# A gated mix of attention and GEGLU: the gate and up products each get a row tile of their own

## The chip, the cores and the metric

The kernel runs on one core of one Trainium2 chip. The metric is the device time of one execution in microseconds (us). Before the change three runs took 1230.1, 1230.26 and 1230.33 us, so the median is 1230.26 us. The core has a matrix engine (TensorE, PE in the profile, with its weight loads shown as PEld), a vector engine (VectorE, DVE), an activation engine (ScalarE, ACT), a general engine (GpSimd, POOL), a queue engine that issues most transfers (SyncE, SP), and two memories on the chip: SBUF, which every engine reads, and PSUM, eight banks into which PE accumulates.

## The reference

x has 2048 rows of 512 numbers. Everything is float32.

```python
g = sigmoid((x * gate_w).sum(-1, keepdims=True))
# attention: 32 query heads of 16, one key and one value head for all of them
q = heads(x @ wq);  k = x @ wk;  v = x @ wv
p = softmax(einsum("bhqd,bkd->bhqk", q, k) * 16 ** -0.5)
a = merge(einsum("bhqk,bkd->bhqd", p, v)) @ wo
# feed-forward, hidden width 1376
b = (gelu(x @ w_gate) * (x @ w_up)) @ w_down
out = g * a + (1 - g) * b
```

The softmax needs 2048 x 2048 exponentials for each of the 32 heads, and all of them go through ACT.

## The kernel before

**Tiles.** The 2048 rows are four groups of 512 (`tg`). The hidden width of the feed-forward is cut into 11 chunks of 128 (`NF`), so there are 44 chunks `n = 11 * tg + r`. Products in which accuracy matters are made from two float32r halves of each operand, high and low: one product is three matmuls, high by high, high by low and low by high. A split is a copy to float32r on DVE (line 186) and a subtraction on POOL (line 187).

**Prologue** (the first 79.5 us). The loads, the splits of x, and for every row group the query, key and value projections and chunk 0 of the feed-forward. The groups run in the order 1, 2, 3, 0. In the last of them (lines 434 to 467) PE makes four query blocks `pq`; for each, `post_q` takes a row maximum (line 272) and the low half (line 281) on DVE. The maxima meet in `pairmax` (lines 470 to 477), whose transposes `pm` stand in PE's queue, and its result `sh` is what the matmul `pb` (line 481) needs. Both are in PE's order ahead of everything that follows.

**Main part.** A step of attention is a score (two 51-row matmuls into one of three two-bank buffers, line 745), an exponential over 128 x 1024 on ACT (line 748) into one of 12 buffers `p`, and, for two scores together, the product with v (line 816, four column tiles of 32, here called a V). There are 1024 scores and 512 V. Between them PE works through jobs of the feed-forward: 39 gate jobs (gate and up of one chunk), 16 down jobs and 6 jobs of the output projection (`wo`). A job fills two PSUM banks: `z`, which is the third score buffer, and `y`.

**Two row tiles.** A job's matmuls contract 128 rows as two halves of 64 rows, one in the lower and one in the upper half of the array, and the two run side by side. `pair_mm` (lines 509 to 531) gives `z` to the lower tile and `y` to the upper tile in the first half of the job, and swaps them in the second. Between the halves stands a relay: a GpSimd nop (line 523) that waits for the last matmuls of the first half, and for which the first matmuls of the second half wait.

**The order of work** is a list written out by hand, `PLAN`, one line per job. H opens the job, F is one pair of its matmuls (Fk is k of them), S is a score into one of two buffers, Z a score into the third buffer (the one that `z` uses between H and R), V is one product with v, R reads the job's banks out, T queues the tanh of a gate job on ACT. The steps go out in this order, and each engine works its own queue in that order.

**Side work** sits in slots: after every third F, `slot` issues one waiting item on DVE and POOL, from `todo` (splits of weights and of x) or, when that is empty or in some slots of a first half, from `bg` (pieces of the softmax's division, `norm`). A gate job of 24 F has seven slots. Items issued in a job's slots stand in DVE's queue ahead of the job's own read-out, which is issued at R: lines 615 and 617 for a down job, line 541 and the GELU chain (lines 544 to 557) for a gate job.

**Batches.** A down job multiplies all chunks collected so far by `w_down`: after chunk 5 and after chunk 10 of each row group, two down jobs each (two blocks of 128 rows in a job), with 18 and 15 terms, so 36 and 30 F. The next row group's x is loaded in four pieces of 128 x 512 and split in the slots of the down jobs after chunk 10. Loads go from SP through a ring of four staging buffers (`st`).

## Time and profile before

| | |
|---|---|
| median of three runs | 1230.26 us |
| the profiled execution | 1230.25 us |
| its span in the trace | 1228.5 us |
| PE busy | 1222.3 us, 9742 matmuls |
| ACT busy | 1025.5 us |
| DVE busy | 545.6 us |
| POOL busy | 216.1 us |
| first score | 79.5 us after the span's start |

The profile shows one execution. The busy time of PE counts modelled ends of pipelined matmuls, so it is the distance between starts that tells what a step costs. A line of the timeline gives start, length, engine, line of the kernel, operation, output and inputs, and a count when equal neighbours are merged; in brackets stands the idle time of the engine before it, and what ended it. A line of a group ends in busy time, mean length of one in ns, and idle time before.

### The profile page before, as it was taken

The numbers are of one execution on the slowest core, as the hardware profiler recorded it, in microseconds if no ns is written. First come the engines' busy times: TensorE is split into PE (matmuls) and PEld (weight loads), VectorE is DVE, ScalarE is ACT, GpSimd is POOL, SyncE is SP. The second block draws the span as 40 slices with busy tenths as digits, with TensorE's granted clock in tenths as the row PEclk, the third lists the DMA queues.
The fourth block names the chain that finished last, engine by engine and source line by source line (L and its number), as shares of the span: only waits on it lengthen the run. The fifth ranks groups of instructions, "written<-read, shape, count | busy, mean of one in ns | idle before, by whom it ended". The sixth has DMA issues, their size and how long they took to land.

```text
span 1228.5 us, 23738 instructions
## 1 busy us (share of the span) xinstructions
PE 1222.3 (99%) x9742; PEld 670.2 (55%) x9742; DVE 545.6 (44%) x812; ACT 1025.5 (83%) x1127; POOL 216.1 (18%) x188
## 2 busy tenths in 40 slices
PE   9999999999999999999999999999999999999998
PEld 7865455555654555455555554654554555545545
DVE  7774423656245051545437152263626244144624
ACT  5459988988898888988888888889888898889883
POOL 5423101222121010212112020121311011012100
PEclk9999999999999999999999999999999999999999
DMA  8642201222121110112112120111211211002000
GB/s 333 215 132 57 67 7 51 66 61 71 33 66 48 44 32 23 52 54 77 56 35 58 48 67 15 47 43 51 83 41 49 74 49 32 23 27 66 15 1 35
DMA packets 39839, 73.91 MB, mean 60 GB/s; under 512 B 5488, under 2 KB 5744, under 8 KB 39728
## 3 DMA queue, kind: packets, MB, share of 16 engines
q1 hardware_dynamic: 39184, 71.32, 18.4%
q8 instruction: 77, 1.26, 0.4%
q0 software_dynamic: 256, 0.79, 0.2%
q10 hardware_dynamic: 288, 0.26, 0.1%
q14 instruction: 34, 0.28, 0.1%
HBM read 57.41 MB, written 14.94 MB: 59 GB/s over the span
## 4 chain that ended last, share of the span: by engine, by line
PE 93%; DVE 0%; ACT 0%; issue 0%
PE acc L816 38%; PE s L745 23%; PE z L515 20%; PE y L515 11%; PE wos L501 1%; PE u L501 0%; DVE acc L627 0%; ACT p L748 0%; PE wof L501 0%; DVE sq L545 0%; DVE sq L544 0%; DVE gs L541 0%; ACT sq L548 0%
## 5 line engine op out<-in xcount | busy, mean ns | idle before, releaser
L748 ACT ACTIVATE p<-s 128x1024 f32<-128x1024 f32 x1024 | 972.3, 1027 | 143.0 <-PE s L745 137.6
L816 PE MATMUL acc<-p,v 128*32 128x512 f32 x4096 | 485.0, 597 | 0.0
L745 PE MATMUL s<-Q,kp 51*128 51x512 f32 x2048 | 384.6, 415 | 0.1
L745 PEld LDWEIGHTS s<-Q,kp 51*128 51x128 f32 x2048 | 183.7, 184 | 215.7 <-ACT p L748 124.3
L816 PEld LDWEIGHTS acc<-p,v 128*32 128x32 f32 x4096 | 114.0, 109 | 250.6 <-issue 242.3
L187 POOL TENSOR_TENSOR gl<-st,gh 128x512 fp32r<-128x512 f32 x80 | 114.0, 1444 | 755.1 <-PE s L745 375.7
L515 PE MATMUL y<-xh,gh 64*128 64x512 f32 x312 | 125.7, 403 | 0.0
L515 PE MATMUL z<-xh,gh 64*128 64x512 f32 x312 | 125.7, 403 | 0.0
L515 PE MATMUL y<-xl,gh 64*128 64x512 f32 x312 | 122.4, 392 | 0.0
L515 PE MATMUL z<-xl,gh 64*128 64x512 f32 x312 | 122.2, 392 | 0.0
L515 PE MATMUL z<-xh,gl 64*128 64x512 f32 x312 | 121.8, 390 | 0.0
L515 PE MATMUL y<-xh,gl 64*128 64x512 f32 x312 | 121.7, 390 | 0.0
L541 DVE COPY gs<-z 128x512 f32<-128x512 f32 x39 | 27.0, 692 | 194.9 <-PE y L515 112.0
L187 POOL TENSOR_TENSOR dl<-st,dh 128x512 fp32r<-128x512 f32 x44 | 57.3, 1304 | 127.1 <-PE s L745 90.0
L515 PE MATMUL z<-dh,hh 64*128 64x512 f32 x176 | 69.5, 395 | 0.0
L515 PE MATMUL y<-dh,hh 64*128 64x512 f32 x176 | 69.5, 395 | 0.0
L515 PE MATMUL y<-dl,hh 64*128 64x512 f32 x176 | 69.0, 392 | 0.0
L515 PE MATMUL z<-dl,hh 64*128 64x512 f32 x176 | 68.8, 391 | 0.0
L515 PE MATMUL z<-dh,hl 64*128 64x512 f32 x176 | 68.7, 391 | 0.0
L515 PE MATMUL y<-dh,hl 64*128 64x512 f32 x176 | 68.7, 390 | 0.0
L515 PEld LDWEIGHTS z<-xh,gh 64*128 64x128 f32 x312 | 58.0, 186 | 15.0 <-POOLq L523 6.8
L515 PEld LDWEIGHTS z<-xl,gh 64*128 64x128 f32 x312 | 58.3, 187 | 8.1
(173 smaller groups left out, 1456.8 us busy)
## 6 DMA issues: line engine op xcount, KB each, us to landing
st<-wf SPq DMA_DIRECT2D x125, 256.0 KB
scr<-q SPq DMA_DIRECT2D x16, 512.0 KB
Q<-scr SPq DMA_DIRECT2D x64, 128.0 KB
Q<-scr SPq DMA_DIRECT2D x64, 64.0 KB
out<-acc SPq DMA_DIRECT2D x16, 256.0 KB
xr<-xT SPq DMA_DIRECT2D x6, 512.0 KB
st<-xT SPq DMA_DIRECT2D x12, 256.0 KB
xr<-xT SPq DMA_DIRECT2D x4, 256.0 KB
```

Of the source, the lines that this page charges most:

```text
L187: eng_l.tensor_sub(lo, src, hi)
L501: nc.tensor.matmul(ps, a, b, start=(first and q == 0), stop=(last and q == len(terms) - 1), skip_group_check=True)
L515: mm = nc.tensor.matmul(ps, a[rs], b[rs], start=(half == 0 and q == 0), stop=(half == 1 and q == len(X) - 1), skip_group_check=True)
L541: nc.vector.tensor_copy(gs, g)
L745: nc.tensor.matmul(ps[:, j * TG : (j + 1) * TG], kp[rs, kc * P : (kc + 1) * P], Q[u][rs, pr], start=True, stop=True)
L748: nc.scalar.activation(p, ps, AF.Exp, bias=0.0, scale=SCALE)
L816: nc.tensor.matmul(accp[u][32 * j : 32 * j + 32], vt[:, kc], pb[s, j // 2][:, (j % 2) * TG : (j % 2 + 1) * TG], start=(kc == 0), stop=(kc ...
```

## The change

- x lies in SBUF twice: for each row group four tiles `xd` hold the same 64 rows of x in partitions 0 to 63 and again in 64 to 127. The gate weights of a chunk lie in the lower 64 partitions, the up weights in the upper. A gate job then has 24 pairs in which the lower tile always makes gate (`z`) and the upper always makes up (`y`): `own_mm`, without the swap and without the relay. Down and wo jobs keep `pair_mm`.
- For row group 0 the doubled x is made in the prologue by 16 copies of 64 x 1024 between partitions, four behind each query block of the last group: one on ACT, one on DVE, two on POOL. For the other groups x is loaded doubled from a new input `xD`, in eight pieces instead of four, and split two pieces to a slot item: the first piece's low half on POOL, the second's on DVE.
- Down jobs come after chunks 3, 7 and 10, so six of them per row group with 24, 24, 24, 24, 18 and 18 F: 24 in all in place of 16.
- Fewer buffers for hidden tiles (`hh`, `hl`: 2 + 2 in place of 3 + 3) and for `w_down` (4 in place of 6). The 12 `p` buffers become 6 pairs. Pools of the prologue are closed in a new order.
- A new list, of 69 jobs. Those around the loads of the next x are shown.

```diff
 PLAN = [
     "t: S2",
...
+    "f: H F3 S F3 S F3 S F3 S F3 S F3 S F3 S F3 R S V S Z T S V6 S",
+    "f: H F3 S F3 S F3 S F3 S F3 S F3 S F4 S F2 R S V3 T S Z S V2 S",
+    "f: H F3 S F6 S2 F6 S F3 R S V Z S2 V3 S",
+    "f: H F3 S F6 S2 F6 S F3 R S V S Z S V3 S2 Z V3 S",
...
+    "f: H F3 S F3 S F3 S F3 S F3 S F3 S F3 S F3 R S V3 T Z S2 V2 S",
+    "f: H F3 S F6 S2 F6 S F3 R S V3 S",
+    "f: H F2 S F4 S F3 S F2 S F4 S F3 R S V Z S2 V3 S2 Z V3 S Z S V2 S",
...
+    "f: H F3 S F3 S F3 S F3 S F3 S F3 S F3 S F3 R S V S Z T S V4 S2 Z V3 S",
+    "f: H F S F8 S2 F7 S F2 R S V2 S Z S V2 S",
+    "f: H F3 S F6 S2 F9 R S2 V2 Z S2 V3 S",
...
+    def big(name):
+        return cp.tile([P, NC, TG], F32R, tag="xr", name=name, bufs=4)
...
+    def xd_tiles(tg):
+        xd[tg] = [[big(f"x{v}{k}{tg}") for k in range(2)] for v in "hl"]
...
-    def split_part(p):
+    def split_part(p, low=nc.gpsimd):
         q, t = raw.pop(0)
         assert p == q
-        split(nc.vector, nc.gpsimd, *target(*p), t)
+        split(nc.vector, low, *target(*p), t)
...
+    def queue_x(tg):
+        ps = x_parts(tg)
+
+        def two(a, b):
+            split_part(a)
+            split_part(b, nc.vector)
+
+        todo.extend(lambda i=i: two(ps[i], ps[i + 1]) for i in range(0, len(ps), 2))
...
+            if last:
+                if b == 0:
+                    xd_tiles(tg)
+                    spread = [(xd[tg][v][k][64 * a : 64 * a + 64, e::2], xs[tg][v][64 * e : 64 * e + 64, 2 * k : 2 * k + 2])
+                              for v in range(2) for k in range(2) for a in range(2) for e in range(2)]
+                for eng in ("a", "d", "p", "p"):
+                    dst, src = spread.pop(0)
+                    if eng == "a":
+                        nc.scalar.copy(dst, src)
+                    else:
+                        (nc.vector if eng == "d" else nc.gpsimd).tensor_copy(dst, src)
...
+    def own_mm(z, y, X):
+        for q, (a, b) in enumerate(X):
+            for lower, ps in enumerate((z, y)):
+                rs = slice(64 * lower, 64 * lower + 64)
+                nc.tensor.matmul(ps, a[rs], b[rs], start=(q == 0), stop=(q == len(X) - 1), skip_group_check=True)
+            if q % EVERY == EVERY - 1 and q + 4 <= len(X):
+                slot(True)
+            yield
...
-            return weights_terms(n, 0), weights_terms(n, 1)
+            assert ("g", n, 1) in done
+            hi, lo = ([w[:, t, c] for t in range(2) for c in range(NC)] for w in G[n])
+            xh, xl = ([x[j // NC][:, j % NC] for j in range(2 * NC)] for x in xd[tg])
+            X = [p for j in range(2 * NC) for p in ((hi[j], xh[j]), (hi[j], xl[j]), (lo[j], xh[j]))]
+            return X, None
...
             if r == NF - 1 and tg + 1 < NTG:
-                queue_parts(x_parts(tg + 1))
+                queue_x(tg + 1)
...
-            if r == 5 or r == NF - 1:
+            if r in (3, 7) or r == NF - 1:
...
-        p = m2.tile([P, 2 * TG], F32, tag="p", name="p", bufs=PB)
-        nc.scalar.activation(p, ps, AF.Exp, bias=0.0, scale=SCALE)
-        pb[s, pr] = p
+        if pr == 0:
+            pb[s] = m2.tile([P, 2, 2 * TG], F32, tag="p", name="p", bufs=PB // 2)
+        nc.scalar.activation(pb[s][:, pr], ps, AF.Exp, bias=0.0, scale=SCALE)
...
-                pairs = pair_mm(z, y, X, Y)
+                pairs = pair_mm(z, y, X, Y) if Y else own_mm(z, y, X)
```

## The prediction

> **What bounds the kernel now.** I read the head of the page, the chain of work that ended last, the busy time by stage, the group of the exponentials, and a stretch of ACT in which six of them ran back to back.

> ```profile
> span 1228.5 us, 23738 instructions
> ...
> PE 93%; DVE 0%; ACT 0%; issue 0%
> ...
> 79.50:1212.00 1132.50, 1132.35 (x9357) 600.15 (x9360) 473.94 (x685) 989.68 (x1065) 182.91 (x134) 1.00 0.16 47
> ...
> L748 ACT ACTIVATE p<-s 128x1024 f32<-128x1024 f32 x1024 | 972.3, 1027 | 143.0 <-PE s L745 137.6
> ...
> 90.62 5.58 ACT L748 ACTIVATE p<-s 128x1024 f32<-128x1024 f32 x6
> ```

> The columns of the stage are its length, then busy time of PE, PEld, DVE, ACT and POOL. PE is never without work for 1132 us, at full granted clock; ACT is idle for 143 us in front of its exponentials, almost all of it waiting for PE's scores, and DVE for 658. So a change is worth what it adds to or takes from the distances between PE's starts. DVE and POOL matter only where PE waits for one of them. The profiled execution took 1230.25 us, 1.75 more than its span and as good as the median of 1230.26. I sum against 1230.25.

> **The relays taken away.** The timeline of PE, around the middle of a gate job, and of the weight loads there:

> ```profile
> 383.88 0.39 PE L745 MATMUL s<-Q,kp 51*128 51x512 f32 x2
> 384.15 0.49 PE L515 MATMUL z<-xh,gh 64*128 64x512 f32 x1
> ...
> 384.49 0.39 PE L515 MATMUL z<-xl,gh 64*128 64x512 f32 x1
> ...
> 384.72 0.39 PE L515 MATMUL z<-xh,gl 64*128 64x512 f32 x1
> ...
> 384.15 0.18 PEld L515 LDWEIGHTS z<-xh,gh 64*128 64x128 f32 x1 [0.31 <-POOLq L523]
> ```

> What to see: a step takes 0.23 us (384.49 to 384.72). The first pair behind the relay starts 0.27 behind the score and the second 0.34 behind the first, because the weights could not be loaded ahead. A relay in plain surroundings costs 0.04 + 0.11 = 0.15 us. In the old list 30 of the 39 gate jobs have it plain ("F3 S" in front); 6 have two scores in front, which cover 0.46 us, and 3 stand behind a V, where the array pays for the V anyway (below). I take 30 x 0.15 = -4.5 us; if none of the others were free it would be -5.9. On POOL the nop leaves the queue, and subtractions that stood behind it go earlier; they are for weights a job ahead, so that is worth nothing.

> **Relays added.** Down and wo jobs go from 22 to 30, each with its relay. In the old list 6 of these are plain, in the new 17: 11 x 0.15 = +1.7 us. The 13 others have two scores or a V in front.

> **The list.** What else it changes on PE is how often V and row-tiled matmuls alternate:

> ```profile
> 389.07 0.96 PE L745 MATMUL s<-Q,kp 51*128 51x512 f32 x6
> 389.96 3.64 PE L816 MATMUL acc<-p,v 128*32 128x512 f32 x32
> 393.54 0.97 PE L745 MATMUL s<-Q,kp 51*128 51x512 f32 x6
> 394.43 2.78 PE L816 MATMUL acc<-p,v 128*32 128x512 f32 x24
> 397.15 0.50 PE L745 MATMUL s<-Q,kp 51*128 51x512 f32 x2
> ```

> Four V take 3.58 us to the next start and three take 2.72, so a V is 0.86 and a group has 0.14 on top; three scores behind a group take 0.89 instead of 0.69. A group costs 0.14 + 0.20, some 0.33 us. F, S and V are as many as before (1608, 1024, 512 steps); groups of V fall from 219 to 214: 5 x 0.33 = -1.7 us. F3 S stays the rhythm, 4 x 0.23 = 0.92 us, and six exponentials in a row took (5.58 - 1.03) / 5 = 0.91 each, so ACT just keeps up when the relay's pause is gone. I cost it at nothing; if that cover fails, each of the 8 scores of a gate job adds the difference, and at 0.95 us each (972.3 / 1024) 39 x 8 x 0.03 = 9 us.

> **The next x, split in the slots.** Before, the four pieces are split in a down job of 30 F:

> ```profile
> 290.88 0.40 PE L515 MATMUL z<-dh,hh 64*128 64x512 f32 x1
> ...
> 290.69 0.69 DVE L770 COPY n<-acc 128x512 f32<-128x512 f32 x1 [4.36 <-PE acc L816]
> 291.29 2.19 DVE L186 CAST xh<-st 128x512 fp32r<-128x512 f32 x3
> 293.40 1.77 DVE L776 SCALAR_TENSOR_TENSOR nz<-n,mk,nz 128x512 f32<-128x512 f32 x1
> ...
> 297.91 1.76 DVE L782 RECIPROCAL nz<-n 128x128 f32<-128x128 f32 x2
> ...
> 299.47 0.39 PE L515 MATMUL z<-dh,hl 64*128 64x512 f32 x1
> ...
> 299.89 0.75 DVE L617 SCALAR_TENSOR_TENSOR acc<-z,gc,acc 128x512 f32<-128x512 f32 x1 [0.22 <-PE z L515]
> 300.56 0.74 DVE L617 SCALAR_TENSOR_TENSOR acc<-y,gc,acc 128x512 f32<-128x512 f32 x1
> ...
> 291.85 4.48 POOL L187 TENSOR_TENSOR xl<-st,xh 128x512 fp32r<-128x512 f32 x3 [14.79 <-PE s L745]
> ...
> L187 DVE TENSOR_TENSOR xl<-xr,xh 128x512 fp32r<-128x512 f32 x15 | 10.3, 700 | 0.0
> ...
> 376.27 0.76 DVE L186 CAST gh<-st 128x512 fp32r<-128x512 f32 x2
> ...
> L186 DVE CAST gh<-st 128x512 fp32r<-128x512 f32 (+1 forms) x81 | 30.7, 419 | 0.0
> ```

> DVE was done 0.22 us before z could be read, 0.42 behind the last pair. And it is slow while POOL subtracts: a cast takes 0.42 and the next starts 0.34 behind it (two in 0.76), but of the three the last took 2.19 - 0.67 = 1.5, until POOL's first subtraction was over (three in 4.48), and nz took 1.77 where an operation with two inputs alone takes 0.70. A new item is cast, cast, and a subtraction on DVE while POOL does the first piece's: 0.67 to its start, POOL's end at 0.55 + 1.35 = 1.9, then about 0.5 more. 2.4 us an item. If nothing blocked, it would be 1.4.

> The new down jobs behind chunk 10 have 18 F and 4 S, 21 x 0.23 = 4.85 us from first to last pair, and three such items (slots behind pairs 3, 12 and 15) are in DVE's queue ahead of the first job's read-out; pairs 6 and 9 issue pieces of the division. What DVE had before that:

> ```profile
> 370.41 0.39 PE L515 MATMUL z<-xh,gl 64*128 64x512 f32 x1
> ...
> 370.84 0.69 DVE L541 COPY gs<-z 128x512 f32<-128x512 f32 x1 [1.01 <-PE z L515]
> ...
> 375.66 0.69 DVE L557 TENSOR_TENSOR hl<-gs,hh 128x512 fp32r<-128x512 f32 x1
> ```

> A gate job followed by "S V3 T" has its GELU done 5.95 us after its last pair. I count from the first pair of the down job; jobs are numbered by the list's lines, with "t" as 0, so the three are 14, 32 and 50.
> - Job 14: the list puts it 6.3 us behind the gate job's last pair, so the splits start at -0.35. Three items (7.2) and two reciprocals left over from the division (0.9 each) end at 8.65, z is read by 9.4. "R S V Z" wants its bank at 4.85 + 0.23 + 0.33 + 0.97 = 6.4. PE waits 3.0.
> - Job 32: three items and the division's last cast and subtraction (1.1) end at 7.95, z is read by 8.7, y by 9.45. There is no Z; the next job wants both banks at 4.85 + 3.6 = 8.45. PE waits 1.0.
> - Job 50: the copy of a finished softmax sum comes first, so x starts at +0.4 (as at 291.29, 0.4 after that job's first pair); three items and two mask products (0.85 each) end at 9.3, z is read by 10.05. "R S V2 S Z" wants it at 4.85 + 2.75 = 7.6. PE waits 2.45.

> Together +6.5 us. With 1.4 us an item all three vanish: 0 is the lower end; with loads that arrive late 8 is the upper. I take 6.5, as the blocked rows are of this very place. The loads themselves (24 of 256 KB in place of 12) need a staging buffer, and a buffer comes free 2 to 3 us ahead of need. SP issues 12 more; only in job 50 do the six loads of Q stand between them.

> **The prologue.** POOL copies eight blocks of 64 x 1024 and DVE four, behind the query blocks:

> ```profile
> 62.92 0.69 DVE L406 SCALAR_TENSOR_TENSOR sqf<-gsf 96x512 f32<-96x512 f32 x1 [0.70 <-ACT gsf L405]
> ...
> 67.73 0.69 DVE L272 TENSOR_REDUCE qmx<-pq 128x1 f32<-128x512 f32 x1 [0.28 <-ACT q L278]
> ...
> 69.79 0.69 DVE L272 TENSOR_REDUCE qmx<-pq 128x1 f32<-128x512 f32 x1 [0.77 <-PE pq L246]
> ...
> 70.60 0.15 DVE L277 TENSOR_REDUCE mm<-kmx 128x1 f32<-128x4 f32 x1
> ...
> 71.63 0.38 PE L473 MATMUL pm<-ident,mm 128*1 128x128 f32 x2
> ...
> 58.29 0.52 POOL L419 MEMSET hl<- 32x512 f32 x1
> ...
> L202 POOL MEMSET kp<- 32x2048 f32 x2 | 3.6, 1798 | 0.3 <-POOLq L921 0.3
> ```

> DVE has 1.05 us idle between 65 and 70 and is 0.9 ahead of pm, which stands in PE's queue. Three copies of 0.76 (two casts) come before pm and one before sh. Unblocked, that costs PE 0.8 us. But POOL, free behind its fill at 58.8, copies from there on, and the GELU of chunk 0 (three operations) and the copies wait behind it as above. No row shows such a copy. A fill takes 0.88 ns an element (1798 / 2048), a subtraction with two inputs 2.9 (4.48 us / 3 / 512); a copy with one input is nearer the fill. At 0.95 us a copy, eight in a row, the waits are 0.5 (line 406), 0.8 (line 407) and 0.9 (the first copy). With 2.3 for the copies, less 1.05 idle and 0.9 ahead, pm is 2.4 late, and sh another 0.6. I take +3.0. The ends are 0.8 and some 12 at the two-input rate, 3 us a copy; midway between the rows, at 1.9, it is about 6.

> [...] No run here shows the copy yet.

> **At nothing.** Eight more read-outs of two banks (1.5 us each) stand in DVE's idle 658 us. Pairs of p free a buffer after the same V as before. Fewer hidden and w_down buffers are reused only after the batch that read them.

> **Sum.** -4.5 + 1.7 - 1.7 + 6.5 + 3.0 = +5.0: 1235.2 us.

> **Rivals.**
> - DVE keeps up, because POOL's work does not hold it up. Speaking for it: the old list never left z waiting. Against: its job had 30 F for the same place. It decides below about 1.5 us an item and with unblocked copies: 1230.25 - 4.5 + 0.8 = 1226.5, faster.
> - Only one of the two bites: 1226.5 + 2.2 = 1228.7 (prologue alone) or 1226.5 + 6.5 = 1233 (jobs 14, 32, 50 alone).
> - The fixed tiles save nothing: the 0.15 us comes from another cause than the swap. Against: the weight loads' row names the relay. 1235.2 + 4.5 = 1239.7.

> **How the numbers follow.** The forecast's case 0.5, DVE keeps up 0.22, one of the two 0.2, no saving 0.08. Three runs lie within 0.23 us; 0.2% or 2.5 us is about what can be told from no change. The first rival is faster; half of the one-sided case and a fifth of the forecast's lie within (0.2); the rest, 0.58, is slower. The range 1226 to 1241 takes in the first rival, the last one, and the forecast with 8 and 6 for its two unknown terms (1239.7); beyond it stay the 3 us copies, an ACT that falls behind, and gains that I do not see, 0.2 in all. The forecast's own range is 1232 to 1240.

> **What the profile will show.** Right: no POOLq release and 0.23 us steps through gate jobs; 17 plain relays at 0.15; in jobs 14 and 50 a Z score waiting for DVE line 617; pm starting near 74 and the first score near 82.5. Wrong: z read 0.43 us after the last pair in job 14, or the first score at 79.5.

## The result

The changed kernel takes 1244.28 us (median; its runs lie between 1242.36 and 1244.99), the kernel before 1230.28 beside it: a ratio of 1.011, 95% interval 1.0099 to 1.0122. It is 14.0 us slower, where 5.0 were forecast. The profiled execution took 1244.99 us with a span of 1243.2, against 1230.25 and 1228.5, so the traces have 14.7 us to explain.

The page of the changed kernel, the lines that answer to those shown of before, and the granted clock by slices of 31 us:

```profile
span 1243.2 us, 23284 instructions
PEclk9999999999899999999999999999989999999999
PE 87%; DVE 5%; ACT 1%; DMA 0%; issue 0%; ACTq 0%; DVEq 0%
L800 ACT ACTIVATE p<-s 128x1024 f32<-128x1024 f32 x1024 | 972.7, 1026 | 146.6 <-PE s L796 145.2
```

DVE now carries 5% of the chain that ended last; it carried none. The exponentials are as long as before (1026 ns in the mean, 1027 before). Two slices of the clock's row (an 8 among nines) are new. The busy time by stage (columns as in the prediction: length, then PE, PEld, DVE, ACT, POOL, granted clock, DMA, GB/s) shows the main part and three short windows in it and before it:

```profile
83.15:1227.97 1144.82, 1135.10 (x9361) 608.99 (x9361) 523.16 (x725) 991.51 (x1065) 187.89 (x134) 0.99 0.17 49
317.40:324.22 6.82, 6.03 (x30) 1.81 (x30) 5.01 (x10) 2.85 (x3) 1.28 (x1) 0.50 0.66 193
914.73:921.56 6.83, 6.21 (x28) 2.30 (x30) 3.53 (x5) 2.53 (x3) 1.39 (x1) 0.50 0.40 115
75.05:78.46 3.41, 3.41 (x10) 2.35 (x9) 2.58 (x8) 1.29 (x3) 0.75 (x1) 0.50 0.46 116
```

The same view of the kernel before, from its first score at 79.49 to the tail:

```profile
79.49:1212.73 1133.24, 1133.09 (x9361) 600.16 (x9360) 473.94 (x685) 989.68 (x1065) 182.92 (x134) 1.00 0.16 47
```

The first score starts 3.66 us later (83.15 against 79.49), the main part is 11.58 longer (1144.82 against 1133.24), and the tail is 0.5 shorter. In these three windows, 17.1 us together, PE was granted half its clock; before, the full clock was granted from 6 us to 1227.97 us, in the tail. A view of the waits, by engine and by what ended them (in total, times, longest):

```profile
PE s L796 <- DVE acc L667: 7.5, 2, 4.5
PEld z L561 <- POOLq L569: 4.2, 14, 0.3
PE pm L510 <- DVE mm L289: 2.0, 1, 2.0
PE y L550 <- DVE gs L598: 1.5, 1, 1.5
```

The relays (POOLq) are left only in down and wo jobs (L561), none in gate jobs (L550). PE waits for DVE in three kinds of places. The first is where the prediction looked, in job 14:

```profile
308.69 0.76 DVE L198 CAST xh<-st 128x512 fp32r<-128x512 f32 x2
309.25 1.35 POOL L199 TENSOR_TENSOR xl<-st,xh 128x512 fp32r<-128x512 f32 x1 [8.16 <-PE s L796]
309.49 1.67 DVE L199 TENSOR_TENSOR xl<-st,xh 128x512 fp32r<-128x512 f32 x1
311.07 1.75 DVE L833 RECIPROCAL nz<-n 128x128 f32<-128x128 f32 x2
...
315.06 0.75 DVE L198 CAST xh<-st 128x512 fp32r<-128x512 f32 x2
...
317.40 0.74 DVE L667 SCALAR_TENSOR_TENSOR acc<-z,gc,acc 128x512 f32<-128x512 f32 x1
...
318.19 1.65 PE L796 MATMUL s<-Q,kp 51*128 51x512 f32 x6 [2.99 <-DVE acc L667]
...
319.77 4.97 PE L867 MATMUL acc<-p,v 128*32 128x512 f32 x24
```

Three items and two reciprocals stand in front of the read-out of z, and the score that wants the bank waits 2.99 us. Then the second loss: 24 matmuls of V, which take 2.8 us at full clock (three took 2.78 in the kernel before), take 4.97. In job 50:

```profile
905.41 0.33 SPq L366 DMA_DIRECT2D st<-xD  x1
905.79 0.42 SPq L393 DMA_DIRECT2D Q<-scr  x1
...
907.66 1.52 SPq L399 DMA_DIRECT2D Q<-shs  x2
...
909.29 1.38 SPq L366 DMA_DIRECT2D st<-xD  x3
...
913.48 0.43 DVE L198 CAST xh<-st 128x512 fp32r<-128x512 f32 x1 [3.92 <-DMA st<-xD]
...
915.35 1.22 PE L796 MATMUL s<-Q,kp 51*128 51x512 f32 x4 [4.50 <-DVE acc L667]
```

SP issues six loads of the next Q between two loads of x. DVE stands 3.92 us before a cast whose load is not there, with the read-out behind it, and PE waits 4.50. In job 32 only 0.16 us is waited. The last place is the start of job 13:

```profile
293.17 0.69 DVE L821 COPY n<-acc 128x512 f32<-128x512 f32 x1 [5.32 <-PE acc L867]
...
294.50 0.69 DVE L598 SCALAR_TENSOR_TENSOR gs<-y,sq 128x512 f32<-128x512 f32 x1
...
295.24 0.49 PE L550 MATMUL y<-xh,gh 64*128 64x512 f32 x1 [1.48 <-DVE gs L598]
```

Line 12 of the list ends "S V S Z T S V6 S". The step that reads the bank y is put off by two scores behind T; the second of them stands behind V6, and so the copy of a finished sum, which has to wait 5.32 us for V6, is ahead of it in DVE's queue.

### The profile page after: what moved, and what is told of

Its sections match the earlier page's. It is cut to its first block, busy times and chain, and to the rows that moved or that the text cites. A ratio compares the mean times of both kernels' runs of the same rounds, so it can differ in the third digit from the quotient of the medians.

```text
span 1243.2 us, 23284 instructions
## 1 busy us (share of the span) xinstructions
PE 1226.1 (99%) x9742; PEld 680.0 (55%) x9742; DVE 600.2 (48%) x856; ACT 1031.0 (83%) x1131; POOL 229.2 (18%) x196
## 4 chain that ended last, share of the span: by engine, by line
PE 87%; DVE 5%; ACT 1%; DMA 0%; issue 0%; ACTq 0%; DVEq 0%
PE acc L867 36%; PE s L796 22%; PE z L550 15%; PE z L561 8%; PE y L561 4%; PE y L550 2%; DVE xl L199 1%; PE wos L538 1%; DVE xh L198 0%; ACT p L800 0%; DMA st<-xD 0%; DVE n L830 0%; DVE nz L827 0%; DVE hl L603 0%; PE u L538 0%; DVE acc L677 0%
## 5 line engine op out<-in xcount | busy, mean ns | idle before, releaser
L800 ACT ACTIVATE p<-s 128x1024 f32<-128x1024 f32 x1024 | 972.7, 1026 | 146.6 <-PE s L796 145.2
L796 PEld LDWEIGHTS s<-Q,kp 51*128 51x128 f32 x2048 | 186.6, 185 | 216.7 <-ACT p L800 110.2
L550 PE MATMUL y<-xh,gh 64*128 64x512 f32 x312 | 123.1, 395 | 1.5 <-DVE gs L598 1.5
L550 PE MATMUL z<-xh,gh 64*128 64x512 f32 x312 | 123.2, 395 | 0.0
L550 PE MATMUL z<-xl,gh 64*128 64x512 f32 x312 | 122.3, 392 | 0.0
L550 PE MATMUL y<-xl,gh 64*128 64x512 f32 x312 | 122.2, 392 | 0.0
L550 PE MATMUL y<-xh,gl 64*128 64x512 f32 x312 | 121.8, 390 | 0.0
L550 PE MATMUL z<-xh,gl 64*128 64x512 f32 x312 | 121.8, 390 | 0.0
L561 PE MATMUL y<-dh,hh 64*128 64x512 f32 x176 | 71.2, 405 | 0.2 <-DVE acc L667 0.2
L561 PE MATMUL z<-dh,hh 64*128 64x512 f32 x176 | 71.2, 405 | 0.0
L199 POOL TENSOR_TENSOR dl<-st,dh 128x512 fp32r<-128x512 f32 x44 | 64.7, 1473 | 24.4 <-DVE dh L198 20.9
L561 PE MATMUL y<-dl,hh 64*128 64x512 f32 x176 | 69.1, 393 | 0.0
L561 PE MATMUL z<-dl,hh 64*128 64x512 f32 x176 | 69.1, 392 | 0.0
L561 PE MATMUL z<-dh,hl 64*128 64x512 f32 x176 | 68.9, 391 | 0.0
L561 PE MATMUL y<-dh,hl 64*128 64x512 f32 x176 | 68.8, 391 | 0.0
L550 PEld LDWEIGHTS z<-xl,gh 64*128 64x128 f32 x312 | 58.4, 187 | 9.8
L550 PEld LDWEIGHTS z<-xh,gl 64*128 64x128 f32 x312 | 57.5, 184 | 10.6
```

The lines of the kernel that those rows point to most:

```text
L199: eng_l.tensor_sub(lo, src, hi)
L550: nc.tensor.matmul(ps, a[rs], b[rs], start=(q == 0), stop=(q == len(X) - 1), skip_group_check=True)
L561: mm = nc.tensor.matmul(ps, a[rs], b[rs], start=(half == 0 and q == 0), stop=(half == 1 and q == len(X) - 1), skip_group_check=True)
L796: nc.tensor.matmul(ps[:, j * TG : (j + 1) * TG], kp[rs, kc * P : (kc + 1) * P], Q[u][rs, pr], start=True, stop=True)
L800: nc.scalar.activation(pb[s][:, pr], ps, AF.Exp, bias=0.0, scale=SCALE)
```

## The experiments

**e1: no next x.** Nothing of groups 1 to 3 is loaded or split.

```diff
-                supply += x_parts(tg + 1)
...
-                queue_x(tg + 1)
+                xd[tg + 1] = xd[tg]
```

> Left out: the x of groups 1 to 3 is neither loaded nor split; all gate jobs use the x of group 0, so the output is not the reference's. Theory (DVE's queue, and the clock that drops behind the stalls): the waits of TensorE in jobs 14 (3.6 us), 32 (0.65) and 50 (5.0) and both windows at half clock in the main part go, about 7.8 + 6.5 us, so 1244.3 becomes about 1230; the granted clock stays at 1.0 from 79 us to 1228 us. Rival (the row tiles and the new list cost time of their own, and the waits only mark it): less than 4 us come back, 1240 or more. Second rival (the waits count, the clock does not): 7.8 come back, about 1236.5.

Measured: 1232.46 us, ratio to the kernel before 1.0015 (1.0005 to 1.0025). 11.8 of the 14 us come back, nearer to the theory (14.3) than to the second rival (7.8); the half-clock windows of the main part are gone, and the wait of job 13 and the late first score (82.7) are still there. (The expectations count a gap from one matmul's start to the next: 3.6, 0.65, 5.0 and 1.9 us stand for the waits of 2.99, 0.16, 4.50 and 1.48 above.)

**e2: the same x work, behind the read-out.** The four items of a group go from the slots to fixed scores after the first down job's R.

```diff
+XLATE = ((1, 4, 7, 10), (3, 5, 10, 13), (1, 4, 9, 12))
...
-        todo.extend(lambda i=i: two(ps[i], ps[i + 1]) for i in range(0, len(ps), 2))
+        xq.extend(lambda i=i: two(ps[i], ps[i + 1]) for i in range(0, len(ps), 2))
...
+            if xq and i == 0:
+                for k in XLATE[tg]:
+                    defer(k, lambda: xq.pop(0)())
```

> Nothing is left out; the four x items of each group are issued behind the first down job's read-out, two to four scores apart, in place of in its slots. Theory (the stall is only the order in DVE's queue): read-outs come first, the three waits and the two windows at half clock go, about 1230, as without any x. Rival (DVE has no room for 4 x 2.4 us near the end of a group, wherever they stand): the wait reappears at the next read-out or at an accumulator's copy, 2 to 5 us each, and the clock drops again, 1238 to 1246.

Measured: 1232.35 us (1.0013; 1.0003 to 1.0022), the same as without any x. PE waits for no read-out of a down job any more; from 313 to 320 us, around the place of job 14's wait, it is busy for all 7.00 us. So the work itself costs nothing that shows; its place in DVE's queue cost it all. The rival, no room on DVE, is out. One thing was not as expected: a half-clock window behind the 1.47 us wait at job 13, where the changed kernel has the same wait and no window.

**e3: T one score earlier in line 12.**

```diff
-    "f: H F3 S F3 S F3 S F3 S F3 S F3 S F3 S F3 R S V S Z T S V6 S",
+    "f: H F3 S F3 S F3 S F3 S F3 S F3 S F3 S F3 R S V S T Z S V6 S",
```

> One letter of the list moves: in line 12 the T stands one score earlier, so that job 13 finds its y bank free. Theory (job 13's first pair waits for an outer that stands behind an accumulator's copy): the 1.9 us gap at 293 us goes and nothing else moves, about -1.6, so 1242.7. Rival (ACT and DVE are as late by then, the wait moves to the next score): 1244.3.

Measured: 1242.21 us, 2.1 less than the changed kernel; the wait at job 13 is gone and those of jobs 14 and 50 stay, at 3.32 and 3.49 us. The window behind job 50 is half as long (3.41 us), so the 2.1 is not the price of the 1.48 alone.

**e4: the prologue's copies as DMAs.**

```diff
+                    if eng in "adp":
+                        nc.sync.dma_start(dst.bitcast(F32), src.bitcast(F32))
```

> The 16 copies that lay the x of group 0 out twice are DMAs on SP's queue, in place of copies on ACT, DVE and POOL. Theory (the copies delay the last reduction on DVE, then pm, then everything): first score back near 79.5 us from 83.15, about -3.7, so 1240.6; the window at half clock near 75 us goes. Rival (16 DMAs of 256 KB go in front of the q stores and of the loads of the first Q on the same queue): first score at 83 us or later, 1244 to 1250.

Measured: 1257.73 us, 13 more than the changed kernel. Half of the theory held: pm starts at 71.63, as before the change. But the rival decided:

```profile
71.63 0.38 PE L512 MATMUL pm<-ident,mm 128*1 128x128 f32 x2
...
86.08 4.17 SPq L503 DMA_DIRECT2D xl<-xl  x4
...
95.56 1.42 PE L798 MATMUL s<-Q,kp 51*128 51x512 f32 x4 [16.00 <-SPq L736]
```

SP is still issuing copies at 86 to 90 us, and the first score waits 16 us for SP to reach the branch (line 736) that all engines take together.

**e5: e2 and e3 together.** 

> Nothing is left out; the late x items and the earlier T of line 12 together. Theory: what each took off alone adds up, 1232.35 - 2.0, about 1230.3, the same as the kernel before; no granted clock under 1.0 between 79 us and the tail. Rival (the 1.9 us gap alone did not matter once the x stalls are gone): 1232.

Measured: 1229.06 us, 0.9989 (0.998 to 0.9998), 1.2 below the sum that was expected; e2's window behind job 13 is gone with the wait.

```profile
81.91:1211.35 1129.44, 1128.81 (x9362) 607.69 (x9361) 524.09 (x726) 991.05 (x1065) 188.16 (x134) 1.00 0.17 50
```

At full clock and with waits of some tenths in all, the main part is 3.8 us shorter than before the change (1133.24). That is what the fixed row tiles and the new list are worth. Against it the changed kernel's main part is 15.4 longer: 9.1 of waits (1.48 + 2.99 + 0.16 + 4.50) and 6.3 that remain for 13.65 us at half clock. That fits: PE was busy for 12.24 us of them (6.03 + 6.21), and half of that, an estimate of the work lost that takes half the clock for half the pace, is 6.1. The changed kernel's trace is of an execution 0.7 us above its median and e5's of one 0.7 us below, so the two lie 1.4 us further apart than the medians.

**e6: e5 with the relay back in each gate job.**

```diff
+                if q == len(X) // 2:
+                    after(mm.ins, relay)
+            if q == len(X) // 2 - 1:
+                relay = nc.gpsimd.nop(nofuse=True).ins
+                for name in behind:
+                    after(relay, name)
```

> Nothing is left out; to the late items and the earlier T, each gate job gets back, in its middle, a relay through POOL between its last pair of the first half and its first of the second. Theory (a relay costs TensorE 0.15 us where it stands, so taking 30 out gave 4.5): 39 x 0.15 = 5.9 if all are plain, 4.5 if 30 are, so 4 to 6 us above the kernel without them (about 1235). Rival (TensorE has slack there, ACT sets the pace, a relay costs nothing): within 1 us of it.

Measured: 1235.2 us (1.0038; 1.0025 to 1.0052), 6.1 above e5. Waits and main part:

```profile
PEld z L553 <- POOLq L558: 11.5, 37, 0.4
```
```profile
83.24:1218.19 1134.95, 1133.86 (x9362) 599.42 (x9361) 524.46 (x725) 995.22 (x1065) 187.88 (x134) 1.00 0.17 50
```

The main part is 5.5 us longer than that of e5, 0.14 for each of 39 relays; the spans differ by 6.8, and the other 1.3 lies in the prologue, where this execution had a half-clock window and that of e5 had none (first score at 83.24 against 81.91). A relay costs PE what the prediction read off the weight loads, and ACT's pace does not cover it.

**e7: e5 with no copy on DVE.** 

> Nothing is left out; to the late items and the earlier T, the four copies of the prologue that stood on DVE go to ACT and POOL (7 and 9 in place of 4 and 8). Theory (DVE's own copies make the last reduction late, 2.2 us): pm at 71.6 to 72 in place of 73.8, no window at half clock near 74 us, first score at 79.5 to 81, so 2 to 4 us less, about 1227. Rival (POOL's copies block DVE, and more of them block more; or ACT's copies hold up the casts of q): pm at 73 or later, 1229 to 1232.

```diff
-                for eng in ("a", "d", "p", "p"):
+                for eng in ("aapp", "aapp", "aapp", "appp")[b]:
```

Measured: 1227.35 us (0.9976; 0.9966 to 0.9986). pm starts at 73.14 instead of 73.78 and the first score at 81.0: between theory and rival. ACT's copies now stand in front of its casts of q, and the row maxima on DVE follow those.

**e8: graded stalls.** DVE gets k idle copies of 0.69 us ahead of the read-out of 16 gate jobs.

```diff
+        for _ in range(PLUG.get(n, 0)):
+            nc.vector.tensor_copy(sq, g)
         nc.vector.tensor_copy(gs, g)
```

> Nothing is left out of the work that is needed; to the late items and the earlier T, 16 gate jobs get 3 to 8 idle copies of 0.69 us on DVE ahead of their read-out, to make stalls of graded length on TensorE, far from each other. Theory (a stall that lasts over about 2 us drops the granted clock to a half for 3.4 or 6.8 us soon after, a shorter one doesn't): gaps up to 1.5 us are followed by no window, gaps from 2.5 us up each by one or two; each window of 3.4 us costs about 1.6 to 3.4 us beside the gap itself. Rival (the windows of the changed kernel come from something else, the x copies or the load on DVE and POOL): no window follows the gaps, and the span is longer by the gaps alone.

Measured: 1303.18 us in its one run, span 1301.4. Four of the scores that waited, in order of time, the total of the waits, and windows at half clock, the first and the last of twelve:

```profile
185.29 0.74 PE L806 MATMUL s<-Q,kp 51*128 51x512 f32 x4 [1.87 <-DVE gs L593]
221.25 0.73 PE L806 MATMUL s<-Q,kp 51*128 51x512 f32 x4 [2.61 <-DVE gs L593]
600.12 0.96 PE L806 MATMUL s<-Q,kp 51*128 51x512 f32 x6 [2.31 <-DVE gs L593]
1109.23 0.97 PE L806 MATMUL s<-Q,kp 51*128 51x512 f32 x6 [1.33 <-DVE gs L593]
```
```profile
PE s L806 <- DVE gs L593: 45.8, 16, 5.2
```
```profile
222.25:225.66 3.41, 3.41 (x20) 0.87 (x16) 2.46 (x5) 2.06 (x3) 0.00 (x0) 0.50 0.00 0
...
1222.36:1229.18 6.82, 6.27 (x28) 1.49 (x28) 5.88 (x10) 3.37 (x4) 1.03 (x1) 0.50 0.00 0
```

The four waits below 2 us (0.25, 1.16, 1.33 and 1.87) are followed by no window, the twelve from 2.31 us up by one each, of 3.41 or 6.83 us, 58.0 us in all. So a long enough stall makes the window without any copy of x ahead of it; the rival is out. Against e5 the span is 74.8 us longer, 45.8 of it waits: up to 29.0 for 58.0 us at half clock, 0.5 us for each.

**e9: e5 with the copies on POOL.**

```diff
-                for eng in ("a", "d", "p", "p"):
+                for eng in ("ppppp", "ppppp", "pppp", "aa")[b]:
```

> Nothing is left out; to the late items and the earlier T, the copies of the prologue go 14 to POOL and 2 to ACT behind its last cast of q; DVE and the casts of q are free of them. Theory (pm was late by the time of the copies that stood on DVE and ACT themselves): pm at 71.6 to 72.2 (73.14 with 7 on ACT and 9 on POOL), first score at 79.5 to 80, about 1226. Rival (POOL's copies block what DVE does beside them): DVE's 0.69 us instructions take up to 1.4 in the prologue, pm at 73 or later, 1227.4 or more.

Measured: 1226.41 us, 0.9971 (0.9959 to 0.9983), the fastest of these kernels and faster than the one before. DVE, and PE's pm and first score:

```profile
63.81 1.41 DVE L436 SCALAR_TENSOR_TENSOR sqf<-sqf,gsf 96x512 f32<-96x512 f32 x1
...
66.46 1.29 DVE L440 SCALAR_TENSOR_TENSOR sqf<-sqf,gsf 96x512 f32<-96x512 f32 x1
...
70.86 0.15 DVE L290 TENSOR_REDUCE mm<-kmx 128x1 f32<-128x4 f32 x1
```
```profile
71.78 0.38 PE L513 MATMUL pm<-ident,mm 128*1 128x128 f32 x2
...
79.64 0.75 PE L803 MATMUL s<-Q,kp 51*128 51x512 f32 x4
```

Two operations of the GELU are blocked by POOL's copies (1.41 and 1.29 in place of 0.69), just as in the changed kernel (1.41 and 1.30), and yet pm is only 0.15 us later than before the change. The rival's blocking is real, but DVE's idle time takes it in as long as no copy stands on DVE; in e7 the copies on ACT made pm late. In the changed kernel the blocking and DVE's own copies use up the same idle time, and no run has DVE's copies without POOL's, so how the 2.16 us divide between them is not shown.

**e10: the changed kernel, with only the loads of Q24 issued later.**

```diff
-        if pr == 0 and kc == 2 and u >= 1 and u + 1 < 8 * NTG:
+        if pr == 0 and kc == (12 if u == 23 else 2) and u >= 1 and u + 1 < 8 * NTG:
```

> Nothing is left out; the kernel as changed, with one thing moved: the loads of Q24 are issued ten steps later, behind the x loads of job 50 on SP's queue. Theory (the forecast of 2.45 us in job 50 became 5.0 because an x load stood behind six Q loads): the gap in job 50 falls to about 2 to 3 us, job 14 and 32 stay, 1242 with as many windows, 1239 to 1241 if a window goes too. Rival (the load was late for other reasons, or DVE alone makes the wait): 4.5 to 5 us stay, 1244.

Measured: 1239.07 us (1.0072; 1.0057 to 1.0088), 5.2 below the changed kernel. In job 50:

```profile
905.26 4.65 SPq L366 DMA_DIRECT2D st<-xD  x4
...
912.14 0.73 PE L796 MATMUL s<-Q,kp 51*128 51x512 f32 x4 [1.44 <-DVE acc L667]
```

Four x loads go out in a row, the wait falls from 4.50 to 1.44, and the 6.83 us at half clock behind it go. Not all of the 5.2 is job 50's: job 14, which the edit leaves alone, waits 2.30 in place of 2.99, because a window at half clock behind job 13 made PE later and DVE's items took as long as before (1417 ns in the mean for a subtraction of x in both).

**e11 and e12: the changed kernel with shorter or other items.** In e11 both subtractions of an item are DVE's, as the diff shows; in e12 the two calls lose `nc.vector`, and both are POOL's.

```diff
-            split_part(a)
-            split_part(b, nc.vector)
+            split_part(a, nc.vector)
+            split_part(b, nc.vector)
```

> Nothing is left out; the kernel as changed, with both subtractions of an x item on DVE and none on POOL, so that nothing blocks DVE's. An item is two casts and two subtractions. Theory (POOL beside it makes DVE's subtraction 1.67 in place of 0.69 us): subtractions at 0.69, item 2.1 in place of 2.37 us, gaps in job 14 and 50 shorter by 0.3 to 0.7 each, 1242.5 to 1244. [...]

> Nothing is left out; the kernel as changed, with both subtractions of an x item on POOL, so that an item is two casts on DVE, 0.8 us or some more. Theory (the stall is the length of the items ahead of the read-out in DVE's queue): the gaps in jobs 14 and 32 go and that of job 50 falls to what the late load leaves, 1 to 4 us, with at most one window left in the main part, 1232 to 1238. Rival (casts that wait for POOL's two subtractions, 2.7 us an item, or for the loads, hold DVE as long): gaps of 3 to 5 us stay, 1242 to 1246.

Measured: 1239.15 us (1.007; 1.0055 to 1.0085) and 1238.09 us (1.0066; 1.005 to 1.0081). DVE's subtractions of x in the changed kernel:

```profile
L199 DVE TENSOR_TENSOR xl<-st,xh 128x512 fp32r<-128x512 f32 x12 | 17.0, 1417 | 0.4
```

and in e11, with its wait in job 14:

```profile
L199 DVE TENSOR_TENSOR xl<-st,xh 128x512 fp32r<-128x512 f32 x24 | 16.6, 692 | 0.8
```
```profile
317.20 1.03 PE L796 MATMUL s<-Q,kp 51*128 51x512 f32 x6 [2.27 <-DVE acc L667]
```

Alone, twice as many subtractions take DVE less time than half of them beside POOL; the item is 2.1 us, and the wait 0.7 shorter, the upper end of what was expected; from the first cast to the read-out DVE takes 8.00 us in place of 8.71. The time itself lies 3.4 us under the range that was expected: a cast of job 50 waits 1.90 us for its load instead of 3.92 and PE 2.71 instead of 4.50, and each of the two windows is 3.41 us long instead of 6.83. By what means POOL holds DVE up is not shown; the traces have 1.67 us for a subtraction beside POOL's in job 14, and 0.69 without. In e12, waits of job 14 and 50:

```profile
316.46 0.97 PE L796 MATMUL s<-Q,kp 51*128 51x512 f32 x6 [0.93 <-DVE acc L667]
...
909.41 1.22 PE L796 MATMUL s<-Q,kp 51*128 51x512 f32 x4 [3.74 <-DVE acc L667]
```

In job 14 the wait falls from 2.99 to 0.93, not to nothing, because two casts now wait 0.99 and 1.09 us for their loads; in job 50 a cast waits 4.25 us for a load behind Q's, and 3.74 are left. The theory of the queue's length holds, and where the items get short, the loads come next.

## Why the prediction was wrong in size

Right in kind, with the number that the runs put beside each:

- Relays and list: -4.5 was forecast for the three terms together (-4.5, +1.7, -1.7); e5 against before gives -3.8. A relay costs 0.14 (0.15 was forecast); the other two terms were not tested apart. ACT kept up: the view of waits gives PE 0.2 us for it in all.
- Job 14: 3.0 forecast, 2.99 measured, from an item of 2.4 us (the reciprocals start 2.38 behind the first item's casts, at 311.07 and 308.69). The second decimal is luck: with the same items the wait was 3.32 in e3 and 2.30 in e10, as PE came earlier or later.
- Prologue: +3.0 forecast, +3.66 measured, near it in part by luck. At full clock the first score is 2.42 late (81.91 in e5 against 79.49), 0.6 less than forecast, and half clock put 1.24 on top. pm was 2.16 late; 2.4 was forecast, though the figures written down for it (0.5 + 0.8 + 0.9 + 2.3 - 1.05 - 0.9) add up to 2.55. A POOL copy took 1.04 to 1.4 us (0.95 taken).

The steps that failed:

- **The clock, which had no term.** "PE is never without work for 1132 us, at full granted clock" was read as a property of the kernel, and it was one of a kernel without waits. Waits forecast at 3.0 and 2.45 us should have had a price for what follows them. It was 6.3 us in the main part, and 1.2 of the prologue's 3.66 (e5's execution had no window there).
- **Job 50**, "only in job 50 do the six loads of Q stand between them", with no us put to it, and "a buffer comes free 2 to 3 us ahead of need": 2.45 forecast, 4.50 measured, and 1.44 in e10, where the loads of Q are out of the way. The count itself was thus 1.0 too high, for the most part because the two mask products took 0.47 and 0.49 us (905.85 and 906.36 in the changed kernel) where 0.85 each were taken. Job 32, costed by the same count at 1.0, waited 0.16.
- **Job 13**, "A group costs 0.14 + 0.20", so that the list was costed by its number of groups. The order within line 12 costs 1.48 us of waiting, which e3 takes away.

From the forecast 5.0 to the 14.7 of the traces: clock of the main part 6.3, job 50 2.05, job 13 1.48, prologue 0.66, list 0.7, job 32 -0.84, tail -0.5, together 9.8, for 9.7 to be explained. The 6.3 is what is left between two traces when their waits are taken off, so the sum closes by the way it is made; that the 6.3 is the clock's rests on the 6.1 worked out under e5 and on e8.

The rival of a DVE that keeps up was forecast to give 1226.5. The changed kernel does not do that; e9, which does the same work in another order, takes 1226.41. So close an agreement is luck: the rival was summed from -4.5 and +0.8, and e9's trace has -3.6 in the main part, +0.15 ahead of it and -0.6 in the tail.

## What to carry to other kernels

Before moving work into a queue, see what stands behind it that another engine wants: the same items (four in each of three groups) cost 12 us ahead of a read-out and nothing behind it. Price a wait of the matrix engine with what follows it: here each us of a wait over 2 us brought another 0.7 to 0.8 at half clock (up to 29.0 for 41.2 in e8, 6.3 for 7.5 in the changed kernel). Look along the queue that feeds the items (SP) as closely as along the one that works them off. A list written by hand can be checked for such places line by line: who reads a bank last, and what stands ahead of that reader.

## What was not expected of the hardware

```profile
71.64:75.05 3.41, 1.46 (x8) 1.09 (x8) 2.89 (x7) 1.44 (x2) 0.00 (x0) 1.00 0.81 279
75.05:78.46 3.41, 3.41 (x10) 2.35 (x9) 2.58 (x8) 1.29 (x3) 0.75 (x1) 0.50 0.46 116
```
```profile
72.07:75.48 3.41, 1.55 (x8) 1.34 (x9) 2.88 (x7) 1.71 (x3) 0.00 (x0) 1.00 0.84 269
75.48:78.89 3.41, 3.21 (x16) 2.22 (x15) 2.92 (x8) 1.03 (x2) 1.03 (x1) 1.00 0.43 123
```

The same wait for pm, 1.96 and 1.9 us long, leaves 1.46 us of PE's work in one cell and 1.55 in the other, where the grid cuts it otherwise: the one is followed by half clock, the other not. So in these traces a wait under 1.9 us was safe but for two cases; one over 3.9 (1.93 in each of two neighbouring cells) would, by an estimate from these counts, drop the clock wherever it lies; and between them it was the grid's chance. All twelve waits of 2.31 us and more in e8 had enough of their length in one cell. Runs of e2 spread over 3.6 us and those of the kernel before over 1.2; that this chance is the reason is not shown. In e2 it fits (six runs with a mean granted clock of 0.997 took 1232.25 to 1233.5 us, the other four, at 0.998 and 0.999, 1229.86 to 1231.99), in e1 it does not (four runs at 0.999 took 1231.74 to 1232.88, five at 0.997 took 1232.44 to 1232.54). The two exceptions are both the wait of 1.47 us at job 13, in e2 and e10; the same wait in the changed kernel and in e1 had no window. What sets them apart stays open.
